# Weight conversions in a spectral mixing stage: six in place of five, their absolute value moved ahead of the relu, matrix loads at other units

## The chip, the core and the metric

The kernel runs on one core of a Trainium2 chip. The metric is the device time of one execution in microseconds (us), the median over several runs. Engines are named as the profile names them: PE (TensorE matmul), PEld (its weight loads), DVE (VectorE), ACT (ScalarE), POOL (GpSimd), SP (SyncE, which here only issues transfers). Every engine works through its own list of instructions in order, and waits on semaphores for the others.

## What is computed

The input is `x` of 2 x 3008 x 256 (batch, sequence, dim). A spectral stage takes a real Fourier transform along the sequence, mixes the 256 channels by one complex matrix with bias, shrinks real and imaginary part softly towards zero, and transforms back. Two feed-forward layers follow.

```python
X = np.fft.rfft(x, axis=1)
Yr = Xr @ w_r - Xi @ w_i + b_r
Yi = Xr @ w_i + Xi @ w_r + b_i
Yr = np.sign(Yr) * np.maximum(np.abs(Yr) - 0.01, 0.0)   # Yi likewise
y = np.fft.irfft(Y, n=x.shape[1], axis=1)
h = y @ w_in;  g = h * sigmoid(1.702 * h);  z = g @ w_out     # 256 -> 2048 -> 256
h = z @ w_in2; g = h * sigmoid(h);          out = g @ w_out2
```

The four feed-forward matrices arrive as 64-bit floats, seen by the kernel as pairs of 32-bit words.

## The kernel before, in words

The work runs in five stages: the forward transform (`fwd`), the mixing (`mid`), the inverse transform (`inv`), and the two feed-forward layers (`mlp`). In all of them the order of each engine's instructions is the order in which the code is written; no scheduler moves them.

**The mixing** has twelve units `i` = 0 to 11 (two batches, two parities of frequency, three blocks of 128 frequencies). PE does a unit into two PSUM banks (`mid_mm`, L539, L542); from unit 2 on that is 25 matmuls of 512 columns, 12 into the first bank, closed by a bias matmul (L545), then 12 into the second. Units from 2 on work on `x` split into a high part `xh` (ACT, L482) and a low part `xl` (ACT, L478, then a POOL-issued transfer that adds, L479). Banks of even units come from pool `ps0`, of odd units from `ps1`, four banks each, so unit `i` needs the banks of unit `i-4` back; the inverse uses the same pools.

Behind PE, one loop pass `i` treats the unit before: ACT copies the first bank to `us` (L551), DVE forms sums and differences of both banks, `sd` (L553 to L555, which frees the banks), ACT applies the relu (L561), DVE finishes the shrinkage `th` (L566), and one pass later DVE folds it to `f` (L578), which the inverse multiplies. The same pass also splits `x` for units `i+2` and `i+3`.

**A weight conversion** (`cv_bits`, L169) turns one 128 x 512 block of 64-bit weights into float32. It has one raw buffer, one work buffer `cv_c`, and these steps: ACT takes the absolute value of the upper words (L175, `cv_c<-raw`), which needs the raw block landed and `cv_c` free again; DVE does five bit operations (L180 to L184); POOL issues a transfer that adds `cv_c` onto `cv_a` in memory (L185), and SP loads the next raw block. `cv_c` is free for the next conversion only when that adding transfer has landed. The DVE and POOL steps wait in a list `fill`, which `pump()` writes out at chosen places. `window(k, done)` places finished blocks (`place_in`, `place_out`: sums on DVE, split into high and low part) and begins `k` new conversions.

Ten of the 32 conversions stand ahead of `mlp`: three in `fwd` (`tf`), those at the units in `tm` in `mid`, those at the steps in `ti` in `inv`. The table `li` says at which units one of the inverse's four matrix pairs (0.8 to 1.2 MB, tiles `m`) is loaded by SP; the fourth is loaded at step 0 of `inv`. SP's list has both these and the raw blocks. Before the change the loop ends, for `i` in `tm`, with placing and beginning a conversion, so that L175 stands behind the relu of pass `i` and its DVE work in pass `i+1`.

**The inverse** has 16 steps (q, b, t). PE does a step (`inv_mm`, L376) into two banks; a step later ACT copies one bank to `eo` (L668) and DVE combines them into `rt` (L672, L676, L406) or adds and subtracts them (L687, L688). The list `pl` says at which steps a converted block, popped from the list `hold`, is placed. The result `yt` is split into `x` blocks for the first feed-forward layer.

**The feed-forward layers** are matmuls L836 (first product, a fast 2 x 2 scheme) and L808 (second product).

Of the kernel before, what the change touches and what calls it, by code (L numbers as in the profile page):

```python
# [8 lines left out]

F32 = mybir.dt.float32  # L10
CFG = {'lv0': 'V', 'lv': 'V', 'dd0': 'VPVVPPPPPVVP', 'dd': 'V', 'ths': 'VVVVPV', 'thf': 'V', 'ivf': 'V', 'cva': 'P', 'pol': 'PPPP', 'pil': 'P', 'mvl': 'PVVP', 'xl': 'V', 'xse': 'V', 'gl': 'VPPPPPPP', 'tf': [6, 10, 13], 'tm': [1, 3, 5, 7, 9], 'ml': [], 'pk': 6, 'ti': [3, 7], 'pi': 4, 'pl': [1, 4, 8, 10, 13], 'kb': [0, 1, 1, 1, 1, 1, 1, 0], 'kr': [0, 1, 0, 1, 0, 1, 1, 0], 'fa': 3, 'xp': [2, 4, 4, 5], 'xq': [1, 4, 1], 'xs': 4, 'xi': [7, 7, 9, 10, 10, 11, 8], 'xsi': 9, 'xo': (0, 1, 6, 2, 3, 4, 5), 'xd': (0, 1, 4, 6), 'ca': 4, 'tl': True, 'fwd': 'all', 'rest0': 'all', 'rest1': 'all', 'last1': 'all', 'inv': 'all', 'mid': 'all', 'last0': 'all', 'thm': 'A', 'gl0': 'PVPVVVPV', 'gl2': 'PPPPPPPP', 'gl3': 'PPPPPPPV', 'xl0': 'VVVVVPV', 'xl1': 'V', 'pre': 13, 'pre2': 0, 'yd': 6, 'lvb': 6, 'mlp': 'all', 'pr': 'V', 'pf': 'V', 'eo': '0111', 'n32': 2, 'li': [8, 10, 11], 'lii': [0], 'xa': 4, 'nhb': 6, 'ddb': 6, 'mlp1': 'all', 'mlp2': 'all'}
NUM = dict(li=[5, 6, 7, 8], n32=2, pk=4, ydp=2, lii=[1, 3], xd=(), ml=[], pl=[], xo=range(7), pi=6, nhb=6, tf=[5, 9, 13], tm=[1, 3, 5, 7, 9, 11], ti=[0, 2, 4, 6, 8, 10, 12, 14, 14, 15, 15], kb=[2] * 8, kr=1, fa=3, fe=2, pm=0, nf=4, lvb=6, ddb=8, ivb=1, eob=1, fsb=6, f1=3, f2=0, fm=[7, 8, 9], fi=[1, 1, 2, 2], pre=13, pre2=1, yd=3, psh=0, ie=[12], xp=[1, 3, 4, 5], xq=[1, 2, 2], xs=5, nw=4, xi=[14, 14, 15, 15], xsi=13, rw=2, ca=4, cc=2, tb=1, tmn=1)

DEF = dict(pr="V", pf="V", lv0="V", lv="VPP", dd0="VVVVVP", dd="VPV", mpl="PV", ths="VP", thf="VVPP", fsl="VP", ivf="PPVV", cva="P", pol="P", pil="P", mvl="V", xl="PPVVPPP", xl0="PPVVPPP", xl1="PPVVPPP", xse="VP", gl="P", gl0="P", gl2="P", gl3="P", wcl="V", thc="V", thm="V")
# [42 lines left out]
def spectral_mlp_kernel(ctx, tc, xin, mfwd, minv, wc, bias, w_in1, w_out1, w_in2, w_out2, outT):  # L57
# [4 lines left out]
    def N(k):  # L62
        return CFG.get(k, NUM[k])
# [102 lines left out]
                nc.sync.dma_start(out=raw[:, :].rearrange("p (r d) -> p r d", r=2), in_=src)  # L166
            loaded.append(((kind, l, p, kept), raw))

    def cv_bits(raw, tag="a"):  # L169
        w = raw.bitcast(U32).rearrange("p (n t) -> p n t", t=2)  # L170
        hf = raw.bitcast(F32).rearrange("p (n t) -> p n t", t=2)[:, :, 1]
        c = cv_p.tile([P, 2 * CU], F32, tag="c", name="cv_c", bufs=1)
        a = cv_p.tile([P, 2 * CU], F32, tag=tag, name="cv_a", bufs=3 if tag == "a" else 1)
        cu, au = c.bitcast(U32), a.bitcast(U32)
        nc.scalar.activation(c, hf, AF.Abs, scale=2.0**-112)  # L175
        ts, stt = nc.vector.tensor_scalar, nc.vector.scalar_tensor_tensor
        band, bor, shl = ALU.bitwise_and, ALU.bitwise_or, ALU.logical_shift_left
# [57 lines left out]
    def settle(now=False):  # L235
        pump()
        ended[:] = []
        for u, (a, c) in bits:
            if not u[3]:
                spilled[u[:3]] = d = dram_p.tile([P, 2 * CU], F32, name=f"w_{u[0]}{u[1]}_{u[2]}")  # L240
                nc.sync.dma_start(out=d, in_=a)
        fresh = [(u, a) for u, (a, _) in bits if u[3]]
        done, added[:] = (added + fresh, ()) if now else (added[:], fresh)
        bits[:] = []
        return done

    def window(k, done, now=False, tag="a"):
        for u, a in done:
            if u[0] == "in":
                sums, puts = place_in(u[1], u[2], a, nc.vector if u[2] == NPR // 2 else "D", sums_tmp)  # L250
                if now:
                    for f in (puts[0], *sums, puts[1]):
                        f()
                else:
                    fill.extend(sums + puts)
            else:
                place_out(u[1], u[2], a, nc.gpsimd if u[2] == NPR - 2 else "D")
        for _ in range(min(k, len(loaded))):
            u, raw = loaded.pop(0)
            bits.append((u, cv_bits(raw, tag)))  # L260

    def tick(k=1):
        window(k, settle(True))
# [327 lines left out]
    for i in range(len(mids)):  # L591
        ps = mid_mm(i)
        sd = mid_sd(*post) if post is not None else None
        xsplit(i + 3, 1)
        xsplit(i + 2, 0)
        if thr is not None:
            mid_fold(*thr)
        if sd is not None:
            thr = mid_relu(*sd)
            pump()  # L600
            thr = mid_th(*thr)
        if i in N('li'):
            load_m()
        post = (i, ps)
        if i in N('tm'):
            ready = settle(True)
            window(0, [r for r in ready if r[0][2] < NPR // 2 and r[0][0] == "in"])
            hold.extend(r for r in ready if r[0][2] >= NPR // 2 or r[0][0] == "out")
            window(1, (), tag="ld" if i == N('tm')[-1] else "a")
    sd = mid_sd(*post)  # L610
    mid_fold(*thr)
    thr = mid_relu(*sd)
    pump()
    mid_fold(*mid_th(*thr))
# [516 lines left out]
```

## Time and profile before

| | us |
|---|---|
| median of 3 runs (lowest, highest) | 1166.54 (1165.54, 1167.99) |
| the profiled execution, own time | 1166.52 |
| its span in the trace | 1164.7 |
| PE busy in the span | 1146.9 |
| ACT / DVE / POOL busy | 774.4 / 629.7 / 477.9 |
| mean granted TensorE clock | 0.995 of full |

The span is what the trace covers; 1.8 us of the execution lie around it. A PE that is busy for 98 per cent of the span still may wait in one place, so the stretch around the edit has to be read by itself. Times in the rows are counted from the span's start: the mixing's matmuls run from 61.9 to 132.9, the inverse's from there to 190, then the feed-forward layers to the end.

### The profile page before, as it was taken

The page shows a single profiled execution, that of the slowest core. Times are in us where ns is not written, and L with a number is a line of the kernel's source. Part 1 is how long each engine was busy: PE and PEld are TensorE (multiplying, and loading weights), DVE is VectorE, ACT ScalarE, POOL GpSimd, SP SyncE. Part 2 cuts the span into 40 slices and gives each one's busy share as a digit, 9 for nine tenths or more (in the row PEclk, how much of TensorE's full clock was granted, in tenths as well). Part 3 has the DMA queues.
Part 4 walks back from the last instruction along what each step waited for, and adds up shares of the span by engine and source line. Part 5 has one row for each costly group of instructions (what it writes and reads, how often), then busy time and mean ns, then how long its engine had stood idle before and what let it go on. Part 6 is the DMA issues. An engine that isn't in the chain of part 4 may idle for free.

```text
span 1164.7 us, 14637 instructions
## 1 busy us (share of the span) xinstructions
PE 1146.9 (98%) x5094; PEld 949.7 (82%) x5094; DVE 629.7 (54%) x1013; ACT 774.4 (66%) x1444; POOL 477.9 (41%) x412
## 2 busy tenths in 40 slices
PE   8999899999999999999999999999999999999998
PEld 6768786887888888888889878888888888888897
DVE  7777798766365474575563553442533523523522
ACT  2576446877677667676677786665766765766755
POOL 1243134454444443444436655333433333433333
PEclk9999899999999999999999999999999999999999
DMA  8777666451121121211220100000000000000000
GB/s 295 179 142 149 149 149 119 109 113 33 49 72 37 36 73 37 60 49 37 72 55 19 55 19 19 1 37 1 1 37 1 30 7 1 37 1 1 37 1 32
DMA packets 39564, 68.49 MB, mean 59 GB/s; under 512 B 3649, under 2 KB 15809, under 8 KB 39490
## 3 DMA queue, kind: packets, MB, share of 16 engines
q1 hardware_dynamic: 26162, 45.51, 11.9%
q0 software_dynamic: 13328, 22.05, 11.2%
q8 instruction: 40, 0.66, 0.2%
q14 instruction: 34, 0.28, 0.1%
HBM read 35.15 MB, written 10.35 MB: 39 GB/s over the span
## 4 chain that ended last, share of the span: by engine, by line
PE 81%; issue 7%; ACT 3%; DVE 3%; DMA 3%; POOL 2%; SPq 0%; POOLq 0%; DVEq 0%; ACTq 0%
PE o L808 40%; PE x L836 35%; PE psf L376 4%; PE psm L539 1%; ACT yt L839 1%; DMA cv_a<-cv_c 1%; DMA wo<-cv_a 1%; POOL xl L479 1%; ACT g L841 1%; DMA raw<-in_x 1%; DVE yt L858 0%; DMA xl<-xt 0%; POOL yt L722 0%; ACT x L747 0%; DVE yt L887 0%
## 5 line engine op out<-in xcount | busy, mean ns | idle before, releaser
L846 POOL TENSOR_TENSOR g<-yt,g 128x512 fp32r<-128x512 f32 (+1 forms) x282 | 362.7, 1298 | 495.8 <-PE x L836 332.0
L808 PE MATMUL o<-g,wo 128*128 128x512 f32 (+1 forms) x2304 | 560.1, 385 | 0.5 <-DMA wo<-cv_a 0.5
L836 PE MATMUL x<-x,wi 128*128 128x512 f32 (+1 forms) x2016 | 498.8, 386 | 3.5 <-ACT yt L877 1.9
L808 PEld LDWEIGHTS o<-g,wo 128*128 128x128 f32 x2304 | 432.4, 188 | 81.5 <-DMA wo<-cv_a 1.0
L836 PEld LDWEIGHTS x<-x,wi 128*128 128x128 f32 x2016 | 377.0, 188 | 80.4 <-ACT yt L877 4.9
L839 ACT ACTIVATE yt<-yt 128x512 f32<-128x512 f32 (+1 forms) x288 | 179.1, 622 | 253.6 <-DVE yt L887 204.8
L841 ACT CAST g<-yt 128x512 fp32r<-128x512 f32 (+1 forms) x384 | 235.1, 612 | 12.2
L887 DVE TENSOR_TENSOR yt<-yt,x 128x512 f32<-128x512 f32 (+1 forms) x96 | 64.7, 674 | 214.3 <-PE x L836 213.7
L858 DVE TENSOR_TENSOR yt<-yt,x 128x512 f32<-128x512 f32 (+1 forms) x96 | 64.8, 675 | 167.1 <-ACT yt L855 165.2
L846 DVE TENSOR_TENSOR g<-yt,g 128x512 fp32r<-128x512 f32 (+1 forms) x102 | 70.1, 687 | 73.2 <-ACT g L841 73.2
L185 POOL DMA_DIRECT2D cv_a<-cv_c x32 | 28.1, 877 | 98.4 <-DVE cv_c L184 92.0
L891 DVE TENSOR_TENSOR yt<-yt,x 128x512 f32<-128x512 f32 (+1 forms) x96 | 64.8, 674 | 0.4 <-issue 0.3
L754 DVE TENSOR_TENSOR x<-yt,x 128x512 fp32r<-128x512 f32 (+1 forms) x44 | 46.2, 1051 | 29.6 <-ACT x L747 29.6
L875 ACT COPY yt<-x 128x512 f32<-128x512 f32 (+1 forms) x96 | 54.7, 570 | 2.9 <-PE x L836 2.9
L839 ACT ACTIVATE yt<-x 128x512 f32<-128x512 f32 (+1 forms) x96 | 56.1, 584 | 0.0
L877 ACT COPY yt<-x 128x512 f32<-128x512 f32 (+1 forms) x96 | 55.7, 580 | 0.1
L376 PE MATMUL psf<-m,xf 128*128 128x190 f32 (+3 forms) x224 | 53.2, 399 | 2.4 <-POOL xf L327 2.4
L376 PE MATMUL psi<-m,f 128*128 128x188 f32 (+3 forms) x224 | 49.0, 373 | 6.2 <-DVE sd L555 2.9
L855 ACT COPY yt<-x 128x512 f32<-128x512 f32 (+1 forms) x96 | 54.7, 570 | 0.0
L376 PEld LDWEIGHTS psf<-m,xf 128*128 128x128 f32 x224 | 39.3, 193 | 16.1 <-POOL xf L327 3.0
L376 PEld LDWEIGHTS psi<-m,f 128*128 128x128 f32 x224 | 39.7, 199 | 13.8 <-DVE sd L555 3.2
L175 ACT ACTIVATE cv_c<-raw 128x512 f32<-128x512 f32 x32 | 21.5, 673 | 19.0 <-DMA cv_a<-cv_c 8.7
(118 smaller groups left out, 817.5 us busy)
## 6 DMA issues: line engine op xcount, KB each, us to landing
raw<-in_wi SPq DMA_DIRECT2D x32, 256.0 KB, 3.7
cv_a<-cv_c POOLq DMA_DIRECT2D x32, 256.0 KB, 5.1
raw<-in_wo SPq DMA_DIRECT2D x16, 512.0 KB, 3.9
xl<-xt POOLq DMA_DIRECT2D x20, 256.0 KB, 4.3
out_t<-yt SPq DMA_DIRECT2D x20, 256.0 KB, 2.0
raw<-in_x SPq DMA_DIRECT2D x9, 512.0 KB, 6.0
w_in<-cv_a SPq DMA_DIRECT2D x8, 256.0 KB, 2.0
w_out<-cv_a SPq DMA_DIRECT2D x8, 256.0 KB, 2.0
```

The source lines that it names most:

```text
L376: nc.tensor.matmul(ps, hi[:, c : c + P], m[:, k, :w], start=i == 0, stop=i == last)
L808: nc.tensor.matmul(acc[h, mm], st, mv, start=first and k == 0, stop=last and k == 2)
L836: nc.tensor.matmul(ps, st, mv, start=first and m == 0, stop=m == 2, skip_group_check=True)
L839: nc.scalar.activation(g, g if src is None else src, func)
L841: nc.scalar.copy(gh, g)
L846: eng.tensor_sub(gl, g, r32(gh))
L855: nc.scalar.copy(y1, X)
L858: nc.vector.tensor_add(y1, y1, Y)
L875: nc.scalar.copy(y2, Z)
L877: nc.scalar.copy(y3, X)
L887: nc.vector.tensor_add(y2, y2, X)
L891: nc.vector.tensor_add(y3, y3, Z)
```

## The change

In the mixing, conversions begin at units 0, 2, 4, 6, 8, 10 in place of 1, 3, 5, 7, 9, and in the inverse at step 3 alone in place of 3 and 7; the total stays at ten ahead of `mlp`. The block that places and begins is moved from the end of the pass to the place between the splits and `mid_fold`. `pump()` runs in every pass, pass 0 too. The sixth conversion writes into a slot of the pool that holds `x`. The first of the placed blocks with index 4 has its low part made by ACT and an adding transfer (`"D"`) in place of two DVE subtractions. The matrices are loaded at units 3, 5, 7 in place of 8, 10, 11. The sixth block is put third in `hold`.

```diff
-CFG = {... 'tm': [1, 3, 5, 7, 9], ... 'ti': [3, 7], ... 'li': [8, 10, 11], ...}
+CFG = {... 'tm': [0, 2, 4, 6, 8, 10], ... 'ti': [3], ... 'li': [3, 5, 7], ...}
...
-    def cv_bits(raw, tag="a"):
+    def cv_bits(raw, n):
...
-        a = cv_p.tile([P, 2 * CU], F32, tag=tag, name="cv_a", bufs=3 if tag == "a" else 1)
+        if n < 4:
+            a = cv_p.tile([P, 2 * CU], F32, tag="a", name="cv_a", bufs=3)
+        elif n == 4:
+            a = cv_p.tile([P, 2 * CU], F32, tag="ld", name="cv_a", bufs=1)
+        else:
+            a = slot(0, F32, "cv_a")
...
-                sums, puts = place_in(u[1], u[2], a, nc.vector if u[2] == NPR // 2 else "D", sums_tmp)
+                sums, puts = place_in(u[1], u[2], a, "D", sums_tmp)
...
         xsplit(i + 3, 1)
         xsplit(i + 2, 0)
+        if i in N('tm'):
+            ready = settle(True)
+            window(0, [r for r in ready if r[0][2] < NPR // 2 and r[0][0] == "in"])
+            hold.extend(r for r in ready if r[0][2] >= NPR // 2 or r[0][0] == "out")
+            window(1, (), n=N('tm').index(i))
         if thr is not None:
             mid_fold(*thr)
         if sd is not None:
             thr = mid_relu(*sd)
-            pump()
+        pump()
+        if sd is not None:
             thr = mid_th(*thr)
         if i in N('li'):
             load_m()
         post = (i, ps)
-        if i in N('tm'):
-            ready = settle(True)
-            window(0, [r for r in ready if r[0][2] < NPR // 2 and r[0][0] == "in"])
-            hold.extend(r for r in ready if r[0][2] >= NPR // 2 or r[0][0] == "out")
-            window(1, (), tag="ld" if i == N('tm')[-1] else "a")
...
     hold.extend(settle(True))
+    hold.insert(2, hold.pop())
```

PE's list of instructions is the same in both, row by row. Three places show what moves. Line numbers of the changed kernel are 5 to 7 higher than before.

First ACT, in passes 9 to 11 of the mixing, from the copy of unit 8's bank to that of unit 11's (`us` is the copy, `th` the relu, `cv_c<-raw` the absolute value that begins a conversion). Before:

```order
L551 COPY us<-psm 128x512
L482 CAST xh<-xt_318 128x512
L482 CAST xh<-xt_319 128x512
L561 ACTIVATE th<-sd,neglam 128x512 x2
L175 ACTIVATE cv_c<-raw_1173 128x512
L551 COPY us<-psm 128x512
L561 ACTIVATE th<-sd,neglam 128x512 x2
L551 COPY us<-psm 128x512
L561 ACTIVATE th<-sd,neglam 128x512 x2
L551 COPY us<-psm 128x512
```

The same passes in the changed kernel:

```order
L556 COPY us<-psm 128x512
L487 CAST xh<-xt_318 128x512
L487 CAST xh<-xt_319 128x512
L566 ACTIVATE th<-sd,neglam 128x512 x2
L556 COPY us<-psm 128x512
L180 ACTIVATE cv_c<-raw_1193 128x512
L566 ACTIVATE th<-sd,neglam 128x512 x2
L556 COPY us<-psm 128x512
L566 ACTIVATE th<-sd,neglam 128x512 x2
L556 COPY us<-psm 128x512
```

The absolute value stood between the relu of pass 9 and the copy of unit 9's bank; it now stands behind that copy and ahead of the relu of pass 10.

Second DVE in the inverse, around the outputs of its second batch (`yt<-rt`) and the first `x` block's preparation. Before:

```order
L718 TENSOR_TENSOR yt<-rt 128x2x187
L180 TENSOR_SCALAR cv_c<-cv_c 128x512
L181 TENSOR_SCALAR cv_c<-cv_c 128x512
L182 SCALAR_TENSOR_TENSOR cv_a<-raw_1478,cv_c 128x512
L183 TENSOR_SCALAR cv_c<-cv_a 128x512
L672 TENSOR_TENSOR rt<-psi,eo 128x2x188
L406 TENSOR_TENSOR rt<-psi,eo 128x2x188
```

The same place in the changed kernel:

```order
L725 TENSOR_TENSOR yt<-rt 128x2x187
L679 TENSOR_TENSOR rt<-psi,eo 128x2x188
L411 TENSOR_TENSOR rt<-psi,eo 128x2x188
L744 TENSOR_TENSOR tmp<-yt 128x512
L745 TENSOR_TENSOR yt<-yt 128x512
```

The second conversion of the inverse is gone from here; a conversion more stands at the start of the mixing instead.

Third SP, from the first matrix load on (`m<-in_mi`; `raw` are the blocks of weights). Before:

```order
L166 DMA raw_1058<-in_wo 128x2x256
L166 DMA raw_1173<-in_wo 128x2x256
L137 DMA m<-in_mi 128x768 x2
L166 DMA raw_1275<-in_wo 128x2x256
L137 DMA m<-in_mi 128x760 x2
L137 DMA m<-in_mi 128x752 x2
L137 DMA m<-in_mi 128x1128 x2
```

The same place in the changed kernel:

```order
L137 DMA m<-in_mi 128x768 x2
L166 DMA raw_954<-in_wo 128x2x256
L137 DMA m<-in_mi 128x760 x2
L166 DMA raw_1075<-in_wo 128x2x256
L137 DMA m<-in_mi 128x752 x2
L166 DMA raw_1193<-in_wo 128x2x256
L166 DMA raw_1292<-in_wo 128x2x256
L137 DMA m<-in_mi 128x1128 x2
```

Three matrix pairs now stand each directly behind a raw block, two raw blocks earlier than before and more.

## Rows read from the trace of the kernel before

**Rows 1.** The page, busy time and share of the span, by engine:

```profile
PE 1146.9 (98%) x5094; PEld 949.7 (82%) x5094; DVE 629.7 (54%) x1013; ACT 774.4 (66%) x1444; POOL 477.9 (41%) x412
```

**Rows 2.** PE's timeline, 132.9 to 197: start, length, operation, idle before and releaser:

```profile
132.91 4.06 PE L376 MATMUL psi<-m,f 128*128 128x192 f32 x24
139.91 2.93 PE L376 MATMUL psi<-m,f 128*128 128x192 f32 x8 [2.94 <-DVE sd L555]
143.30 1.64 PE L376 MATMUL psi<-m,f 128*128 128x190 f32 x4 [0.46 <-DMA m<-in_mi]
...
162.93 15.65 PE L376 MATMUL psi<-m,f 128*128 128x188 f32 x72 [1.27 <-DVE rt L406]
179.32 1.54 PE L376 MATMUL psi<-m,f 128*128 128x188 f32 x8 [0.74 <-DVE rt L406]
181.69 4.06 PE L376 MATMUL psi<-m,f 128*128 128x376 f32 x12 [0.82 <-DVE rt L688]
185.93 0.96 PE L836 MATMUL x<-x,wi 128*128 128x512 f32 x3 [0.19 <-ACT eo L668]
...
195.25 2.34 PE L836 MATMUL x<-x,wi 128*128 128x512 f32 x9 [0.85 <-DVE yt L887]
```

**Rows 3.** Windows: length, then busy by engine, granted clock, DMA share, GB/s:

```profile
139.91:148.94 9.03, 8.57 (x35) 8.06 (x35) 8.93 (x16) 2.93 (x6) 0.00 (x0) 0.66 1.01 338
148.94:161.66 12.72, 12.72 (x79) 12.43 (x78) 11.72 (x25) 4.01 (x7) 3.41 (x3) 1.00 0.18 36
...
162.93:178.58 15.65, 15.65 (x72) 12.16 (x72) 14.98 (x30) 10.87 (x21) 9.84 (x10) 1.00 1.12 187
```

**Rows 4.** PE's timeline, the bias matmul of unit 9:

```profile
118.60 0.39 PE L545 MATMUL psm<-bias_hl,ones 128*128 128x512 f32 x1
```

**Rows 5.** ACT's timeline in the mixing, absolute values and one copy:

```profile
71.27 0.66 ACT L175 ACTIVATE cv_c<-raw 128x512 f32<-128x512 f32 x1
...
116.76 0.67 ACT L175 ACTIVATE cv_c<-raw 128x512 f32<-128x512 f32 x1 [2.58 <-DMA cv_a<-cv_c]
...
130.96 0.66 ACT L175 ACTIVATE cv_c<-raw 128x512 f32<-128x512 f32 x1 [4.52 <-DMA cv_a<-cv_c]
131.53 0.57 ACT L551 COPY us<-psm 128x512 f32<-128x512 f32 x1
```

**Rows 6.** DVE's timeline at the end of the mixing and in the inverse:

```profile
134.60 0.42 DVE L180 TENSOR_SCALAR cv_c<-cv_c 128x512 f32<-128x512 f32 x1
...
136.70 0.69 DVE L184 SCALAR_TENSOR_TENSOR cv_c<-raw,cv_c 128x512 f32<-128x512 uint32 x1
...
139.44 0.42 DVE L555 TENSOR_TENSOR sd<-psm,us 128x256 f32<-128x256 f32 x1
...
142.18 0.68 DVE L553 TENSOR_TENSOR sd<-us,psm 128x512 f32<-128x512 f32 x1
...
148.63 0.55 DVE L676 TENSOR_TENSOR rt<-psi,eo 128x380 f32<-128x380 f32 x1
...
154.44 0.55 DVE L110 TENSOR_TENSOR wi<-cv_a,wi 128x384 fp32r<-128x384 f32 x1
...
162.33 0.55 DVE L406 TENSOR_TENSOR rt<-psi,eo 128x376 f32<-128x376 f32 x1
```

**Rows 7.** POOL's timeline, adding transfers of conversions:

```profile
60.90 0.85 POOL L185 DMA_DIRECT2D cv_a<-cv_c  x1 [0.65 <-DVE cv_c L184]
...
111.25 0.86 POOL L185 DMA_DIRECT2D cv_a<-cv_c  x1 [4.47 <-DVE cv_c L184]
...
123.50 0.86 POOL L185 DMA_DIRECT2D cv_a<-cv_c  x1 [3.03 <-DVE cv_c L184]
137.69 0.86 POOL L185 DMA_DIRECT2D cv_a<-cv_c  x1 [13.32 <-DVE cv_c L184]
```

**Rows 8.** SP's timeline, the first matrix load:

```profile
123.69 0.47 SPq L137 DMA_DIRECT2D m<-in_mi  x1
```

**Rows 9.** Groups by line, one of the four sums of a placed block:

```profile
L213 DVE TENSOR_TENSOR tmp<-cv_a 128x128 f32<-128x128 f32 x8 | 2.3, 285 | 0.5 <-DMA cv_a<-cv_c 0.5
```

More of the change, by code (lines that the diff above doesn't have):

```diff
@@ L10 @@
 F32 = mybir.dt.float32
-CFG = {'lv0': 'V', 'lv': 'V', 'dd0': 'VPVVPPPPPVVP', 'dd': 'V', 'ths': 'VVVVPV', 'thf': 'V', 'ivf': 'V', 'cva': 'P', 'pol': 'PPPP', 'pil': 'P', 'mvl': 'PVVP', 'xl': 'V', 'xse': 'V', 'gl': 'VPPPPPPP', 'tf': [6, 10, 13], 'tm': [1, 3, 5, 7, 9], 'ml': [], 'pk': 6, 'ti': [3, 7], 'pi': 4, 'pl': [1, 4, 8, 10, 13], 'kb': [0, 1, 1, 1, 1, 1, 1, 0], 'kr': [0, 1, 0, 1, 0, 1, 1, 0], 'fa': 3, 'xp': [2, 4, 4, 5], 'xq': [1, 4, 1], 'xs': 4, 'xi': [7, 7, 9, 10, 10, 11, 8], 'xsi': 9, 'xo': (0, 1, 6, 2, 3, 4, 5), 'xd': (0, 1, 4, 6), 'ca': 4, 'tl': True, 'fwd': 'all', 'rest0': 'all', 'rest1': 'all', 'last1': 'all', 'inv': 'all', 'mid': 'all', 'last0': 'all', 'thm': 'A', 'gl0': 'PVPVVVPV', 'gl2': 'PPPPPPPP', 'gl3': 'PPPPPPPV', 'xl0': 'VVVVVPV', 'xl1': 'V', 'pre': 13, 'pre2': 0, 'yd': 6, 'lvb': 6, 'mlp': 'all', 'pr': 'V', 'pf': 'V', 'eo': '0111', 'n32': 2, 'li': [8, 10, 11], 'lii': [0], 'xa': 4, 'nhb': 6, 'ddb': 6, 'mlp1': 'all', 'mlp2': 'all'}
+CFG = {'lv0': 'V', 'lv': 'V', 'dd0': 'VPVVPPPPPVVP', 'dd': 'V', 'ths': 'VVVVPV', 'thf': 'V', 'ivf': 'V', 'cva': 'P', 'pol': 'PPPP', 'pil': 'P', 'mvl': 'PVVP', 'xl': 'V', 'xse': 'V', 'gl': 'VPPPPPPP', 'tf': [6, 10, 13], 'tm': [0, 2, 4, 6, 8, 10], 'ml': [], 'pk': 6, 'ti': [3], 'pi': 4, 'pl': [1, 4, 8, 10, 13], 'kb': [0, 1, 1, 1, 1, 1, 1, 0], 'kr': [0, 1, 0, 1, 0, 1, 1, 0], 'fa': 3, 'xp': [2, 4, 4, 5], 'xq': [1, 4, 1], 'xs': 4, 'xi': [7, 7, 9, 10, 10, 11, 8], 'xsi': 9, 'xo': (0, 1, 6, 2, 3, 4, 5), 'xd': (0, 1, 4, 6), 'ca': 4, 'tl': True, 'fwd': 'all', 'rest0': 'all', 'rest1': 'all', 'last1': 'all', 'inv': 'all', 'mid': 'all', 'last0': 'all', 'thm': 'A', 'gl0': 'PVPVVVPV', 'gl2': 'PPPPPPPP', 'gl3': 'PPPPPPPV', 'xl0': 'VVVVVPV', 'xl1': 'V', 'pre': 13, 'pre2': 0, 'yd': 6, 'lvb': 6, 'mlp': 'all', 'pr': 'V', 'pf': 'V', 'eo': '0111', 'n32': 2, 'li': [3, 5, 7], 'lii': [0], 'xa': 4, 'nhb': 6, 'ddb': 6, 'mlp1': 'all', 'mlp2': 'all'}
 NUM = dict(li=[5, 6, 7, 8], n32=2, pk=4, ydp=2, lii=[1, 3], xd=(), ml=[], pl=[], xo=range(7), pi=6, nhb=6, tf=[5, 9, 13], tm=[1, 3, 5, 7, 9, 11], ti=[0, 2, 4, 6, 8, 10, 12, 14, 14, 15, 15], kb=[2] * 8, kr=1, fa=3, fe=2, pm=0, nf=4, lvb=6, ddb=8, ivb=1, eob=1, fsb=6, f1=3, f2=0, fm=[7, 8, 9], fi=[1, 1, 2, 2], pre=13, pre2=1, yd=3, psh=0, ie=[12], xp=[1, 3, 4, 5], xq=[1, 2, 2], xs=5, nw=4, xi=[14, 14, 15, 15], xsi=13, rw=2, ca=4, cc=2, tb=1, tmn=1)
@@ L245, in settle, with window @@
         return done
-    def window(k, done, now=False, tag="a"):
+    def window(k, done, now=False, n=0):
         for u, a in done:
             if u[0] == "in":
-                sums, puts = place_in(u[1], u[2], a, nc.vector if u[2] == NPR // 2 else "D", sums_tmp)
+                sums, puts = place_in(u[1], u[2], a, "D", sums_tmp)
                 if now:
@@ L259, in window @@
             u, raw = loaded.pop(0)
-            bits.append((u, cv_bits(raw, tag)))
+            bits.append((u, cv_bits(raw, n)))
     def tick(k=1):
```

## The prediction, as it was put on record

> **What bounds the kernel now.** I read the page first: PE is busy for 98% of the span, all other engines for two thirds or less [rows 1]. PE's list of instructions is untouched, so the change can only alter how long PE stands still, or at which clock it runs. PE's own timeline says where that is. Between the mixing's last matmul (132.9) and the first feed-forward matmuls (195) it stops seven times [rows 2]. The largest stop is at the seam: the second step of the inverse waits 2.94 us for DVE's L555, the last op that reads unit 10's banks, and then 0.46 for a matrix. Later it waits 1.27 and 0.74 for L406, 0.82 for L688, 0.19 for ACT's `eo` copy, and 0.85 for L887. After the 2.94 us of idling the granted clock falls to a mean of 0.66 of full over 139.91 to 148.94, part of it at 1.2 in place of 2.4 GHz [rows 3]. There 35 matmuls took 8.57 us; in the next window 79 of nearly the same width took 12.72, 0.161 each, so 35 should take 5.64 and the slow clock cost 2.93.
>
> **Why DVE is late at the seam.** In PE's row for unit 9 the first bank is complete at 118.60 + 0.39 = 118.99 [rows 4]. ACT copies it at 131.53, 12.5 us later, though the copy waits for nothing but its turn: right ahead stands L175, the absolute value, idle for 4.52 us until an adding transfer has freed `cv_c` [rows 5]. Behind that copy come unit 9's sums, folds, and on DVE the five conversion ops from 134.60 to 136.70 + 0.69 = 137.39, the shrinkage, and unit 10's sums, done at 139.44 + 0.42 = 139.86 [rows 6]. PE starts at 139.91. DVE leaves the mixing at 148.63 and is then busy without a break (14.98 of 15.65 us in 162.93 to 178.58, [rows 3]); the 1.27, 0.74 and 0.82 are its lateness carried on.
>
> **The new rhythm.** A conversion round is: absolute value 0.66, the DVE ops 2.79, 0.30 until POOL issues at 137.69, then a tail until the next absolute value may run. Where that one waited for the tail, it was 5.51 (111.25 to 116.76) and 7.46 (123.50 to 130.96) [rows 5, 7]. Before, another 3.64 stood inside the round (130.96 to 134.60): the copy, sums and folds queued between the absolute value and L180. The change puts these ahead of the absolute value, so they can run while it waits. A round thus costs 9.26 to 11.21, mid 10.24, against two PE units of 11.36 (from 118.60 to 132.91 are 63 matmuls, 2.52 units, so 5.68 each).
>
> Six absolute values are five rounds. The first needs the last forward conversion's transfer, issued at 60.90 [rows 7]: 66.4 to 68.4 by the same tails, and at most 71.27, when it ran without waiting [rows 5]. I take 68.4. Two rounds carry the four sums of a placed block, 4 x 0.285 = 1.14 each [rows 9]. The sixth is then at 68.4 + 51.2 + 2.3 = 121.9; with all tails long and the late start 71.3 + 56.1 + 2.3 = 129.7. The tail I choose is the mean of the two, because three of five rounds have matrix loads beside them: the long tail had one, issued at 123.69 [rows 8], the short one none.
>
> What the Trainium skill says of this speaks against the change: "DMA: Bandwidth & Descriptors", section "Queues, rings and completion order", has each transfer engine serve its queues in turn, packet by packet, so a matrix load on SP's queue shares time with POOL's adding transfer beside it and does not wait behind it. The two tails agree with it, without proving it. By it the three rounds with matrices would take the long tail and the rest the short one, 68.4 + 52.2 + 2.3 = 122.9.
>
> **When it is early enough.** From the absolute value to unit 10's sums done there is 0.66 + (139.86 - 134.60) = 5.92, and from there to DVE's first op of the inverse 148.63 - 139.86 = 8.77, the same ops as before: the inverse begins on DVE 14.69 behind the sixth absolute value. It cannot begin before unit 11's own sums allow: they need PE's last matmul (132.9), and took 148.63 - 142.18 = 6.45 to get there, so 139.4. The tightest need of PE behind it is the second half of step 8 (8 of its 16 matmul rows stand before the 1.27 us stop, 8 behind), which waits for the last reader of a bank of step 4: done at 162.33 + 0.55 = 162.88, that is 14.25 into DVE's inverse. The subtractions that leave DVE (0.55 for 384 columns, the second for 512 not shown, about 0.7, less overlap: 1.1) make that 13.15. PE running freely is there at 132.91 + (8 x 16 + 8) x 0.161 = 154.8. So DVE must begin by 141.6, and the sixth absolute value must run by 127.0. My 121.9 leaves 5.1 us, the floor of 139.4 leaves 2.2. Each microsecond past 127.0 costs one.
>
> Steps 13 and 14, where PE waited 0.74 and 0.82 for the readers of steps 9 and 10, get slack from the removed conversion: its five ops (2.8 us) stood on DVE among those readers. The 0.46 for the matrix goes because its load now stands on SP behind the raw block that pass 2 asks for, and not where it was issued at 123.69. The 0.19 goes with the rest, as the ACT copy follows PE and DVE.
>
> **Edits costed at nothing.** The conversion in pass 0 adds 1.14 + 2.79 = 3.9 us of DVE, and the ACT work of a placed block, while PE does units 0 and 1; PE first feels it if unit 3's splits or unit 4's banks (those of unit 0) come late, units later. In4's low part goes to a transfer that is not needed until the fifth feed-forward group. The sixth block's slot is taken from one of `x`'s early units, all read by then, and given back at step 8. If one of these covers fails, the cost is a wait of PE in the mixing, up to some microseconds, which I hold in the range. The 0.85 for L887 stays: it is the feed-forward layer's own chain.
>
> **Sum.** 2.94 + 0.46 + 2.93 + 1.27 + 0.74 + 0.82 + 0.19 = 9.35 us. The profiled execution took 1166.52, the median is 1166.54, so nothing is to be scaled: 1166.5 - 9.35 = 1157.2.
>
> **Rivals.** *Late rounds (0.14).* If all tails are long, the sixth absolute value is at 129.7, 2.7 past the point: 1159.9. For it: the matrices' 2.3 MB move from the seam into the mixing. Against: even so PE's first stop (unit 10's sums, at 135.6 in place of 139.86) is gone.
>
> *Gain given back in the inverse (0.10).* The transfers are at a share of 1.12 in 162.93 to 178.58 [rows 3] and nearly the same ones must pass while PE is 9 us quicker. They start earlier by as much as DVE does (148.63 - 139.4 = 9.2), so they have no room to spare; if `x` blocks then come 2 to 3 us late, 1159 to 1160.
>
> *Slower (0.05).* The rounds do not shorten: four rounds from 71.27 to 130.96 are 14.92 each, and now there are five. The sixth absolute value would be at 68.4 + 74.6 = 143.0, 16.0 past the point: 1173.2, more if the clock falls again. For it: each absolute value waited for a transfer, which moving it does not make faster. Against: 3.64 of the last round was queue, not transfer. It decides from rounds of about 13.6 us (68.4 + 5 x 13.6 = 136.4, 9.4 past the point) on.
>
> *No change (0.03).* Losses and gains within 0.2% of each other, 2.3 us, which is about what a measurement here can tell from nothing.
>
> **The numbers.** Forecast 0.68, which with the late rounds and the give-back makes faster by over 0.2% 0.91; same 0.04, slower 0.05. Range: the low end takes away the 0.85 too, and 0.4 for run spread, 1155.9; the high end takes in the late rounds with 0.7 for a tail longer than the two seen, 1160.6. Outside lie the slower cases, no change, and bits of the rest, about 0.15 to 0.2.
>
> **What would show it.** Right: no stop of PE between 132.9 and 139; granted clock 1.00 in 140 to 149; sixth absolute value before 127.0; DVE's first L676 op (then L683) near 139.5; first feed-forward matmuls near 176.6 in place of 185.93; PE's timeline after that the same, shifted by 9.35. Wrong: rounds above 11.4 us; stops of PE for L406 at step 8; a stop in the mixing around units 3 to 5 for `xh` or `xl`; `x` matmuls waiting for transfers.

## The result and the profile after

The changed kernel takes 1155.38 us in the median of 4 runs (1154.44 to 1156.45). Beside it the kernel before took 1167.26 (1165.54 to 1168.42). The ratio is 0.9900, with a 95% interval of 0.9882 to 0.9918: faster by about 1%, 11.9 us by the medians. The forecast was 1157.2 with a range of 1155.9 to 1160.6, so direction and place came as forecast, and the gain was larger than the range allowed. The profiled execution of the changed kernel took 1156.45 (span 1154.6), 10.07 less than that of the kernel before.

The page of the changed kernel, busy time by engine (to be read beside [rows 1]):

```profile
PE 1141.8 (99%) x5094; PEld 946.6 (82%) x5094; DVE 629.1 (54%) x1011; ACT 775.7 (67%) x1446; POOL 478.8 (41%) x414
```

PE's timeline of the changed kernel over the stretch of [rows 2], from the first matmul of the inverse to the wait for the `x` sums:

```profile
133.26 6.01 PE L381 MATMUL psi<-m,f 128*128 128x192 f32 x36
...
142.63 6.97 PE L381 MATMUL psi<-m,f 128*128 128x190 f32 x42
...
152.95 22.68 PE L381 MATMUL psi<-m,f 128*128 128x190 f32 x106
175.18 1.14 PE L843 MATMUL x<-x,wi 128*128 128x512 f32 x3
...
184.69 2.33 PE L843 MATMUL x<-x,wi 128*128 128x512 f32 x9 [0.85 <-DVE yt L894]
```

Of seven stops one is left, the 0.85 for L894 (L887 before). From the first row to that last one it takes 184.69 - 133.26 = 51.43 us; before it was 195.25 - 132.91 = 62.34 [rows 2]. I call this "the stretch" below. It is 10.91 shorter. The profiled execution of the changed kernel began the stretch 0.35 later, and by the difference of the own times lost 0.49 more behind it: 10.91 - 0.35 - 0.49 = 10.07.

To see where the 10.91 lie, the stretch is cut at four places that are the same in PE's list. Windows of the kernel before (columns as in [rows 3]: the first figure behind the window is its length, the third from the end the granted clock):

```profile
132.91:148.94 16.03, 12.63 (x60) 11.83 (x58) 15.79 (x30) 5.41 (x9) 0.86 (x1) 0.79 0.65 209
148.94:162.93 13.99, 12.72 (x79) 12.43 (x78) 12.96 (x28) 4.01 (x7) 3.72 (x3) 1.00 0.26 46
162.93:185.93 23.00, 21.25 (x92) 15.61 (x92) 22.12 (x43) 15.63 (x31) 15.46 (x16) 1.00 1.11 195
185.93:195.25 9.32, 8.47 (x30) 5.45 (x30) 7.99 (x16) 5.59 (x10) 3.25 (x4) 1.00 0.77 133
```

The same four pieces of PE's list in the changed kernel:

```profile
133.26:142.63 9.37, 9.37 (x60) 9.37 (x59) 8.31 (x15) 3.17 (x6) 0.21 (x1) 1.00 0.30 113
142.63:155.19 12.56, 12.56 (x80) 12.56 (x80) 12.18 (x28) 4.94 (x9) 6.36 (x7) 1.00 0.66 98
155.19:175.18 19.99, 19.99 (x93) 15.59 (x93) 17.70 (x34) 13.86 (x27) 13.26 (x15) 1.00 1.04 181
175.18:184.69 9.51, 8.66 (x33) 5.52 (x31) 7.91 (x16) 5.40 (x10) 3.54 (x5) 1.00 0.66 107
```

Saved: 6.66 at the seam (forecast 2.94 + 0.46 + 2.93 = 6.33), 1.43 around step 8 (forecast 1.27), 3.01 in the rest of the inverse (forecast 0.74 + 0.82 + 0.19 = 1.75), and 0.19 lost in the last piece, at the matmuls right behind the cut. The clock is 1.00 throughout. Each of the first three pieces gave back more than its visible idle time; over the whole stretch it is 10.91 - 9.35 = 1.56 us more.

ACT's timeline of the changed kernel, the absolute values of the six conversions (beside [rows 5]):

```profile
67.07 0.68 ACT L180 ACTIVATE cv_c<-raw 128x512 f32<-128x512 f32 x1 [0.68 <-DMA raw<-in_wi]
...
78.14 0.68 ACT L180 ACTIVATE cv_c<-raw 128x512 f32<-128x512 f32 x1 [2.20 <-DMA raw<-in_wi]
...
90.33 0.67 ACT L180 ACTIVATE cv_c<-raw 128x512 f32<-128x512 f32 x1 [0.64 <-DMA raw<-in_wi]
...
102.05 0.68 ACT L180 ACTIVATE cv_c<-raw 128x512 f32<-128x512 f32 x1 [1.00 <-DMA cv_a<-cv_c]
...
114.30 0.66 ACT L180 ACTIVATE cv_c<-raw 128x512 f32<-128x512 f32 x1 [1.85 <-DMA cv_a<-cv_c]
...
122.97 0.67 ACT L180 ACTIVATE cv_c<-raw 128x512 f32<-128x512 f32 x1 [1.48 <-DMA cv_a<-cv_c]
```

And POOL's, the adding transfers of the first five (beside [rows 7]):

```profile
70.88 0.86 POOL L190 DMA_DIRECT2D cv_a<-cv_c  x1 [0.64 <-DVE cv_c L189]
...
83.18 0.86 POOL L190 DMA_DIRECT2D cv_a<-cv_c  x1 [0.64 <-DVE cv_c L189]
...
94.13 0.86 POOL L190 DMA_DIRECT2D cv_a<-cv_c  x1 [4.32 <-DVE cv_c L189]
106.47 0.86 POOL L190 DMA_DIRECT2D cv_a<-cv_c  x1 [5.30 <-DVE cv_c L189]
118.09 0.86 POOL L190 DMA_DIRECT2D cv_a<-cv_c  x1 [5.52 <-DVE cv_c L189]
```

The rounds are 11.07, 12.19, 11.72, 12.25 and 8.67, where the four rounds of before were 14.92 in the mean. The sixth absolute value runs at 122.97. From a POOL row to the next ACT row it is 7.26, 7.15, 7.92, 7.83 and 4.88. The last three of these ended with the adding transfer; the third and fourth have a matrix load beside them, the fifth has none. The first two ended with the landing of the raw block (`raw<-in_wi` in ACT's rows), and the first of them has no matrix load beside it.

DVE's timeline of the changed kernel, its first operation of the inverse and the last reader of step 4's banks:

```profile
139.99 0.55 DVE L683 TENSOR_TENSOR rt<-psi,eo 128x380 f32<-128x380 f32 x1
...
152.63 0.55 DVE L411 TENSOR_TENSOR rt<-psi,eo 128x376 f32<-128x376 f32 x1
```

The reader is done at 153.18; PE comes to the second half of step 8 at 155.19, so there are 2.01 us to spare. (The expectations below say 155.03 and 1.85, which is one matmul too early: 155.19 is the 137th of the inverse, as 162.93 is in [rows 2].)

### The profile page after: what moved, and what is told of

Read it like the earlier page. It is cut to its first block, busy times and chain, and to the rows that moved or that the text cites. A ratio compares the mean times of both kernels' runs of the same rounds, so it can differ in the third digit from the quotient of the medians.

```text
span 1154.6 us, 14648 instructions
## 1 busy us (share of the span) xinstructions
PE 1141.8 (99%) x5094; PEld 946.6 (82%) x5094; DVE 629.1 (54%) x1011; ACT 775.7 (67%) x1446; POOL 478.8 (41%) x414
## 4 chain that ended last, share of the span: by engine, by line
PE 94%; ACT 2%; DVE 1%; issue 1%; DMA 1%; POOL 0%; SPq 0%; POOLq 0%; DVEq 0%
PE o L815 42%; PE x L843 37%; PE psm L547 5%; PE psf L381 4%; PE psi L381 4%; PE psm L544 1%; ACT yt L846 1%; DMA raw<-in_x 1%; ACT x L754 0%; DVE yt L865 0%; DMA wo<-cv_a 0%; DVE x L761 0%; ACT g L848 0%; ACT yt L862 0%; PE psm L550 0%
## 5 line engine op out<-in xcount | busy, mean ns | idle before, releaser
L894 DVE TENSOR_TENSOR yt<-yt,x 128x512 f32<-128x512 f32 (+1 forms) x96 | 64.8, 675 | 214.3 <-PE x L843 213.8
L381 PE MATMUL psi<-m,f 128*128 128x188 f32 (+3 forms) x224 | 45.1, 357 | 0.0
L754 ACT CAST x<-tmp 128x512 fp32r<-128x512 f32 (+1 forms) x36 | 22.1, 613 | 17.4 <-DVE tmp L763 15.8
```

What stands on the lines that cost most here:

```text
L381: nc.tensor.matmul(ps, hi[:, c : c + P], m[:, k, :w], start=i == 0, stop=i == last)
L894: nc.vector.tensor_add(y2, y2, X)
```

## The experiments

All are edits of the changed kernel unless said otherwise; none changes what is computed. "The stretch" is read in each trace as above (51.43 in the changed kernel; 51.42 in its second trace).

**The changed kernel twice more**, as the level for the others.

> The changed kernel itself, as the level for the others on the same chip. Both theories: 1155.4 us give or take 1.0. If the 1.6 us beyond the forecast were only the luck of the first comparison, the difference to the kernel before should now come near 9.4 us; if they are lost around the stops in time that the profile does not count as idle, near 11 us (10.9 in the two traces between the mixing's last matmul and the wait for the x sums, 11.1 between the fastest runs).

> The changed kernel itself, as the level of this chip for the other two: 1154.4 to 1156.5, in two levels by the granted clock at the start.

Measured: 1154.47 (1154.38 to 1154.68) against 1167.3 for the kernel before, ratio 0.9898 (0.9883 to 0.9912); and 1154.88 (1154.45 to 1156.15) against 1167.48, ratio 0.9897 (0.9881 to 0.9914). So the excess over the forecast was no luck of one comparison: by medians the gain is 11.9 to 12.8 us.

**The place undone.**

```diff
         xsplit(i + 2, 0)
-        if i in N('tm'):
-            ready = settle(True)
...
             thr = mid_relu(*sd)
-        pump()
-        if sd is not None:
+            pump()
             thr = mid_th(*thr)
...
         post = (i, ps)
+        if i in N('tm'):
+            ready = settle(True)
...
```

> Everything of the change but the place: the six conversions begin at the end of the pass again, behind the relu, and the fill list is written out where it was. Theory (the place in ACT's and DVE's lists sets the length of a round): rounds of about 14.9 us as before, the sixth absolute value at 68.4 + 5 x 14.9 = 143, the sums of unit 10 5.9 us later at 149, PE stops for them from about 137 on, 10 to 12 us, and the granted clock falls again: about 1173 us, slower than before. Rival (one conversion less in the inverse, the earlier start and the moved matrices bring the gain, the place does not): 1155 to 1158 us.

Measured: 1166.06 (1164.18 to 1168.32), ratio to the kernel before 0.9991 (0.9980 to 1.0002), no difference beyond the noise. The whole gain is lost without the place. The expected time, 1173, was 7 us too long. ACT's timeline of this kernel shows the rounds and the queue (`us` is the copy of a finished bank):

```profile
124.99 0.66 ACT L180 ACTIVATE cv_c<-raw 128x512 f32<-128x512 f32 x1 [4.57 <-DMA cv_a<-cv_c]
125.56 0.57 ACT L556 COPY us<-psm 128x512 f32<-128x512 f32 x1
...
136.59 0.66 ACT L180 ACTIVATE cv_c<-raw 128x512 f32<-128x512 f32 x1 [1.93 <-DMA cv_a<-cv_c]
137.15 0.57 ACT L556 COPY us<-psm 128x512 f32<-128x512 f32 x1
```

The first four rounds are 14.99, 15.03, 14.25 and 14.23, as the theory says, but the fifth only 11.60, so the sixth absolute value runs at 136.59 and not at 143. The two last tails, from POOL's issue on, are 7.50 (117.49 to 124.99, a matrix load issued at 117.69) and 4.87 (131.72 to 136.59, none), which is the 2.63 by which the fifth round is shorter. The matrix load is not all that differs: two adding transfers of `xl` also stand behind the first of the two (118.03) and none behind the second. It is in matrices_late, below, that a matrix load alone is put beside the last tail. PE's stops in its timeline:

```profile
137.77 3.60 PE L381 MATMUL psi<-m,f 128*128 128x192 f32 x20 [2.38 <-ACT us L556]
...
145.53 0.59 PE L381 MATMUL psi<-m,fd 128*128 128x190 f32 x2 [0.96 <-DVE sd L560]
...
151.77 7.69 PE L381 MATMUL psi<-m,f 128*128 128x192 f32 x28 [3.38 <-DVE rt L411]
```

PE's first stop now ends with the copy that stands right behind the late absolute value (137.15 + 0.57 = 137.72, PE at 137.77): the queue, not the conversion's own work, holds it up. Windows of the same kernel:

```profile
137.00:141.00 4.00, 3.23 (x19) 3.11 (x20) 3.21 (x7) 2.58 (x5) 0.00 (x0) 1.00 0.00 0
150.00:154.00 4.00, 2.23 (x7) 2.23 (x8) 3.31 (x9) 1.30 (x3) 0.86 (x1) 0.60 0.24 99
```

After the stop of 2.38 the clock stayed at 1.00, after that of 3.38 it fell.

**The place alone.**

```diff
-'tm': [0, 2, 4, 6, 8, 10], 'ti': [3],    'li': [3, 5, 7]
+'tm': [1, 3, 5, 7, 9],     'ti': [3, 7], 'li': [8, 10, 11]
-                sums, puts = place_in(u[1], u[2], a, "D", sums_tmp)
+                sums, puts = place_in(u[1], u[2], a, nc.vector if u[2] == NPR // 2 else "D", sums_tmp)
-    hold.insert(2, hold.pop())
```

> The place alone: the five conversions of before at units 1, 3, 5, 7, 9 and two in the inverse, matrices at units 8, 10, 11, the DVE subtractions kept; only where a conversion begins and where the fill list is written out are as in the changed kernel. Theory: the fifth absolute value runs near 71.3 + 4 x 11 = 115, long before the seam, so the 2.94 us stop, the slow clock and the stop at step 8 go; the removed conversion is back on DVE in the inverse (2.8 us) and may bring back 0.7 to 1.6 us around steps 13 and 14: 1155.4 to 1158. Rival (it takes the conversion out of the inverse, or the matrices out of the seam): 1161 us or more.

Measured: 1156.71 (1156.25 to 1158.30), ratio 0.9918 (0.9904 to 0.9932), 10.6 us faster than the kernel before beside it. Its PE timeline has two stops besides that for the `x` sums:

```profile
171.10 4.06 PE L381 MATMUL psi<-m,f 128*128 128x376 f32 x12 [0.82 <-DVE rt L694]
175.35 0.98 PE L842 MATMUL x<-x,wi 128*128 128x512 f32 x3 [0.19 <-ACT eo L674]
...
184.70 2.34 PE L842 MATMUL x<-x,wi 128*128 128x512 f32 x9 [0.85 <-DVE yt L893]
```

The seam is clean; the inverse's second conversion brings back the stop of step 14. No stop for a matrix came back, though the loads are at their old units. The stretch is 184.70 - 131.33 = 53.37, 1.95 longer, though the profile counts only 1.01 as idle. So the place is worth 10.6 of 12.8 us by the medians. The rest comes with the other edits together; of these, the matrices and the subtractions cost nothing clear in the time when undone alone (below), which leaves the sixth conversion. The place in ACT's list and the place in DVE's move together in this edit, and no run parts them.

**Six conversions, each a unit later.**

```diff
-'tm': [0, 2, 4, 6, 8, 10]
+'tm': [1, 3, 5, 7, 9, 11]
```

> The changed kernel with the six conversions at units 1, 3, 5, 7, 9, 11 in place of 0, 2, 4, 6, 8, 10. Theory: the first absolute value at about 71.3, rounds as in the changed kernel (56 us for five), the sixth at about 127, at the point from which on PE waits; behind it fewer sums are queued than I counted, so 1155.4 to 1157. Rival (the earlier start by a unit is what the gain rests on): 4 to 5 us of it are lost, 1159 to 1161 us.

Measured: 1156.57 (1154.59 to 1156.95), ratio 0.9909 (0.9892 to 0.9925). The sixth absolute value ran at 128.31, 1.3 us past the prediction's 127.0, and yet there was no stop at step 8; DVE began the inverse at 140.49, 12.18 behind it and not 14.69. The stretch was 51.95, with one stop of 0.19: the delay of a whole unit costs 0.5 us. The rest of the distance of the medians stands ahead of the stretch, which in this trace begins at 132.86 (131.35 in the changed kernel's second trace). The rival's 4 to 5 us aren't there.

**The matrices back at their old units.**

```diff
-'li': [3, 5, 7]
+'li': [8, 10, 11]
```

> The changed kernel with the matrix loads back at units 8, 10, 11. Theory (they only free the seam of the 0.46 us wait, and lie beside long tails wherever they are): the rounds with units 3 to 7 get shorter by up to 3 us each, the sixth absolute value comes before 122, PE then either waits again about 0.5 us for a matrix near the seam or not at all, since the raw blocks ahead of them on SP now come earlier too: the time within 1 us of the changed kernel's (1154.4 to 1156.4). Rival (moving the matrices carries a good part of the gain, as loads beside the seam hold up the conversions there): 1158 us or more.

Measured: 1154.97 (1154.28 to 1156.72), ratio 0.9898 (0.9883 to 0.9913), and a stretch of 51.42. Moving them brought nothing, once the raw blocks come earlier. But the rounds did not get shorter by up to 3 us each, as I had expected. ACT's timeline of this kernel:

```profile
78.86 0.67 ACT L180 ACTIVATE cv_c<-raw 128x512 f32<-128x512 f32 x1 [2.15 <-DMA raw<-in_wi]
...
89.59 0.68 ACT L180 ACTIVATE cv_c<-raw 128x512 f32<-128x512 f32 x1 [0.16 <-DMA cv_a<-cv_c]
...
100.69 0.66 ACT L180 ACTIVATE cv_c<-raw 128x512 f32<-128x512 f32 x1
...
112.10 0.68 ACT L180 ACTIVATE cv_c<-raw 128x512 f32<-128x512 f32 x1
...
123.85 0.68 ACT L180 ACTIVATE cv_c<-raw 128x512 f32<-128x512 f32 x1 [4.08 <-DMA cv_a<-cv_c]
```

The three rounds that lost their matrix load take 10.73, 11.10 and 11.41, shorter by 1.46, 0.62 and 0.84. The last, with a load issued at 116.46 beside its tail, takes 11.75, longer by 3.08; its tail is 7.58 (from POOL's issue at 116.27) in place of 4.88, and the sixth absolute value runs at 123.85 and not before 122. The absolute values at 100.69 and 112.10 waited for no transfer. Their distance is 11.41, two units of PE (11.36): a conversion stands two passes behind the last, each of these passes begins with the copy of a bank and with splits of `x` that wait for PE (0.72 and 0.73 ahead of 100.69), and so a short tail is not used. The last pass with a conversion has no `x` left to split, and there a late round can catch up: the 8.67 of the changed kernel.

**The subtractions back on DVE.**

```diff
-                sums, puts = place_in(u[1], u[2], a, "D", sums_tmp)
+                sums, puts = place_in(u[1], u[2], a, nc.vector if u[2] == NPR // 2 else "D", sums_tmp)
```

> The changed kernel with the low part of the first block with index 4 made by two DVE subtractions again (about 1.1 us of DVE in the inverse). Theory: in the changed kernel's trace the reader of step 4 is done at 153.18 and PE comes to it at 155.03, 1.85 us later, so 1.1 us more on DVE costs nothing: within 0.5 us of the changed kernel. Rival (the point is tighter, and this edit is a needed part of the gain): 1 us or more is lost in one stop at step 8.

Measured: 1155.05 (1154.53 to 1156.81), ratio 0.9900 (0.9885 to 0.9916), the same as the changed kernel; the stretch is 52.08, 0.66 longer, with one stop of 0.19 for ACT's `eo`, none at step 8. The slack at step 8 is as read; the cost came at the end of the inverse.

**Needless work on DVE ahead of the inverse**: six, then nine additions.

```diff
     mid_fold(*mid_th(*thr))
+    wt = tmp()
+    for _ in range(6):                   # 9 in the second kernel
+        nc.vector.tensor_add(wt, ft[0, 0, 0, 0], ft[0, 0, 0, 0])
```

> The changed kernel with six additions of 512 columns that nobody needs (0.69 us each, 4.1 in all) on DVE ahead of its first operation of the inverse. Theory, first part: the slack at step 8 is 1.85 us, so PE gets one stop of about 2.3 us there. Second part: a stop costs more than the idle time that the profile gives, by 0.16 to 0.4 us, so the stretch from the inverse's first matmul to the wait for the x sums grows by 2.4 to 2.7 (51.43 to about 54.0). The granted clock stays at 1.00, as it did after a stop of 2.38 in the kernel with the old place. Rival to the first: DVE is not what PE waits for there, nothing changes. Rival to the second: the stretch grows by just the idle time shown.

> As the kernel with six needless additions on DVE, but nine of them (6.2 us). With six, the stretch from the inverse's first matmul to the wait for the x sums grew from 51.42 to 55.30, by 3.88, of which the profile counted 2.65 as idle. Theory: from here on each microsecond on DVE costs one, so three additions more (2.07) make it 57.4, if no single stop is long enough for the granted clock to fall; the rise of the first stop (0.35) and that at step 8 (1.49) share it. If one stop comes to 3 us, as at the seam before, the clock falls to 0.50 for some microseconds and the stretch is 60 to 61. Rival (a fixed price per stop, nothing in proportion): 55.3 to 56.

With six: 1159.10 (1157.86 to 1160.17). PE's timeline of that kernel:

```profile
131.21 6.01 PE L381 MATMUL psi<-m,f 128*128 128x192 f32 x36
...
143.35 4.81 PE L381 MATMUL psi<-m,f 128*128 128x192 f32 x28 [0.35 <-DVE rt L411]
...
155.41 16.90 PE L381 MATMUL psi<-m,f 128*128 128x188 f32 x80 [1.49 <-DVE rt L411]
172.93 4.06 PE L381 MATMUL psi<-m,f 128*128 128x376 f32 x12 [0.62 <-DVE rt L698]
177.18 0.97 PE L846 MATMUL x<-x,wi 128*128 128x512 f32 x3 [0.19 <-ACT eo L678]
...
186.51 2.35 PE L846 MATMUL x<-x,wi 128*128 128x512 f32 x9 [0.85 <-DVE yt L897]
```

Four stops, not one, of 0.35 + 1.49 + 0.62 + 0.19 = 2.65 in all. The stretch is 55.30, 3.88 longer, at a clock of 1.00. So 1.23 us are lost without being shown as idle. Set beside the changed kernel's second trace start by start, each of the four stops delays PE by 0.27 more than its idle time, and the remaining 0.14 lies at two matmuls in front of which no idle time is shown. The second part of the theory holds, and the rival that only the idle time counts falls. Of the first part the place holds (L411 at step 8, the largest), the count does not.

With nine: 1162.29 (1159.79 to 1165.23), a stretch of 57.53 where 57.4 was expected for an undisturbed clock. But the clock fell all the same, so the agreement does not confirm the reasoning. PE's one large stop:

```profile
147.27 6.49 PE L381 MATMUL psi<-m,f 128*128 128x192 f32 x28 [2.54 <-DVE rt L411]
```

and a window behind it:

```profile
148.00:150.00 2.00, 2.00 (x8) 2.00 (x7) 1.93 (x7) 0.69 (x3) 0.86 (x1) 0.50 0.03 5
```

Here the stop at step 8 is gone. One reading is that PE at 1.2 GHz came to step 8 late enough that DVE was done, so slow clock and stop stood in for each other; the trace is consistent with that, no run held the clock apart.

**The start.** The profiled executions of the changed kernel differ ahead of the stretch. A window of the changed kernel's first trace:

```profile
12.00:14.00 2.00, 2.00 (x4) 1.00 (x3) 1.51 (x3) 0.51 (x3) 0.42 (x5) 0.50 1.07 405
```

The same window of its second trace:

```profile
12.00:14.00 2.00, 2.00 (x8) 1.21 (x7) 1.15 (x3) 0.64 (x4) 0.20 (x4) 1.00 1.02 395
```

In the first PE ran 4 matmuls there at half clock, in the second 8, and the stretch began at 133.26 and 131.35; the own times are 1156.45 and 1154.42. Two kernels add warming matmuls: seven more ahead of the first pair (the first two lines of the diff), or five between the first pairs (the rest).

```diff
-    for _ in range(13):
+    for _ in range(20):
         nc.tensor.matmul(warm[:, :P], ones_f, ones_f, start=True, stop=True)
...
+    between = [3, 2]
...
+            for _ in range(between.pop(0) if i and between else 0):
+                nc.tensor.matmul(warm[:, :P], ones_f, ones_f, start=True, stop=True)
```

> The changed kernel with 20 in place of 13 warming matmuls at the start. This is about the spread of the runs: the changed kernel's executions come at 1154.4 and at 1156.4, and in the traces the second kind has a granted clock of 0.50 over 12 to 14 us while the first has 1.00. Theory (what differs is the start, where PE stands idle between the first blocks): the warming, some 3 us longer, fills the idle time up to the second pair of matmuls at 8.5 to 9.3, the clock stays at 1.00, and all executions are near 1154.4, or up to 1 us more where the first matmuls come late. Rival (the two levels come from elsewhere): both are still there, or the time is 1 to 3 us longer.

> The changed kernel with three warming matmuls between the first and the second pair of matmuls at the start, and two between the second and the third, where PE stood idle for 0.9 to 2.8 and 0.5 to 1.1 us. Theory (the two levels of the changed kernel, 1154.4 and 1156.4, are the granted clock at the start, which falls after these pauses): clock 1.00 over 10 to 16 us, and all executions between 1154.2 and 1155.2. Rival (the level does not hang on the pauses; a longer warming ahead of the first pair left executions at 1155.3 and 1156.2): the spread stays at about 2 us. If the inserted matmuls come late themselves, up to 1 us is added to all.

Measured: 1154.61 (1154.17 to 1156.16) and 1154.50 (1154.15 to 1154.97), ratios 0.9894 and 0.9893 with intervals that cover the changed kernel's. With the longer warming the higher executions are still there; with the one between the pairs they were absent in 4 runs, which the unedited kernel also did once. That the start makes the levels is shown by the traces; that the pauses alone decide it is not: one_unit_later lost the clock after pauses of 1.08 and 0.51, after_third kept it after 2.77 and 0.57.

The same five matmuls in the kernel before:

> The kernel before with the same five warming matmuls between the first pairs at the start. In all runs so far the kernel before lies between 1164.6 and 1170.6 us, the changed one between 1154.3 and 1156.7. Theory (the changed kernel varies by its start alone; the kernel before varies by its start and by up to 4 us at the seam, where the stops and the slow clock hang on when transfers land): with the start held at clock 1.00 its lowest time stays at 1164 to 1165, its highest falls by about 2 to 1168 or 1169, so it still spreads over 3 us or more, and its median comes to 1165 to 1167. Rival (all of its spread is the start, too): all executions within about 1 us, near 1164.5.

Measured: 1166.27 (1164.63 to 1167.70), against 1167.38 (1165.61 to 1170.35) without. The spread stays at 3.1 us, so it is not the start's alone. In its trace the stretch begins 1.15 earlier than in the other trace of before (131.76), and the wait for the `x` sums ends at 195.18, only 0.07 earlier. The lead was not lost at the seam: PE comes to the second half of step 8 at 161.26, 1.67 earlier than the 162.93 of [rows 2]. It was lost behind that, where the clock fell after stops of 1.06 (at 178.09) and 0.82:

```profile
180.45 5.67 PE L378 MATMUL psi<-m,f 128*128 128x376 f32 x12 [0.82 <-DVE rt L691]
```

```profile
180.00:182.00 2.00, 1.55 (x3) 0.97 (x4) 1.93 (x5) 0.09 (x2) 1.56 (x2) 0.58 1.01 266
```

The same row took 4.06 in the other trace [rows 2]. So the two ends agree by chance. That the seam is what spreads the kernel before, as the theory has it, these two traces do not show: the seam's piece, cut as above, takes 16.03 in one and 16.36 in the other (131.76 to 148.12).

## Why the gain was larger than forecast, step by step

*The cause of the stall* (the place of the conversion, with its absolute value ahead of the copy in ACT's queue) was right, and shown: undoing the place alone takes away the whole gain, the place alone brings 10.6 of 12.8 us.

*The rhythm*: the sixth absolute value was forecast at 121.9 and measured at 122.97, by errors that cancel. The first came 1.33 earlier (67.07 for 68.4). From each absolute value to POOL's issue the five rounds take 20.86 together, forecast 5 x 3.75 + 2.3 = 21.05. The tails behind POOL's issue take 35.04 together, forecast 5 x 6.485 = 32.43 (the mean of 5.51 and 7.46), because four were long and one short. What I missed is the raw block: it ended the first two rounds, at 7.26 and 7.15, and the sum has no term for it. Three of the rounds lay above 11.4, which the prediction calls a sign of being wrong; it cost nothing here, as the sixth absolute value still had 4 us to spare. What the Trainium skill says of queues served in turn ("DMA: Bandwidth & Descriptors", section "Queues, rings and completion order") agrees with the tails that end with the adding transfer, 7.92, 7.83 and 4.88, and with 7.58 where a matrix load was moved beside the last one in matrices_late. By it I had worked out 122.9; that the trace gives 122.97 is luck, as it has four long tails where I counted three, and the earlier start.

*The point from which lateness costs* was right for DVE (by 141.6): DVE began at 139.99, and the measured reader and PE put the point at 139.99 + 2.01 = 142.00, with the inverse begun 0.35 later. For the absolute value (by 127.0) it was too early: in one_unit_later 128.31 brought no stop at step 8, because DVE's work behind it took at most 12.18 and not 14.69. The rival of late rounds did not come, nor did the transfers give anything back: their share is 1.04 over 155.19 to 175.18, and no `x` block was late. The slower rival is refuted with its price: even with the old place it is 1166. There the rounds were as long as feared, but for the last.

*Edits costed at nothing*: the conversion in pass 0, the slot of `x` and in4's transfer cost PE nothing in the mixing, which has no stop. The matrices' move was worth nothing, where I had given it the 0.46.

*The step that failed is the sum.* It priced a stop at the idle time in front of PE's row. In running work the next matmul starts before the last has ended: groups by line and form of the changed kernel give

```profile
L381 PE MATMUL psi<-m,f 128*128 128x188 f32 x88 | 15.5, 322 | 0.0
```

322 ns for one (the profile models the ends), while 42 of nearly that width take 6.97, (6.97 - 0.32) / 41 = 0.162 from one start to the next. The profile counts idle time from the end of the last matmul, 0.16 after the next one should have started, and behind a stop the second start is late as well. PE's timeline of the kernel before has two matmuls behind the stop of 1.27 as

```profile
162.93 0.59 PE L376 MATMUL psi<-m,f 128*128 128x188 f32 x2 [1.27 <-DVE rt L406]
```

and that of the changed kernel two in running work as

```profile
140.70 0.48 PE L381 MATMUL psi<-m,f 128*128 128x188 f32 x2
```

Both pairs end with a matmul of 0.32, so the second start lies 0.27 behind the first in one pair and 0.16 in the other. Set beside each other start by start, the two traces give 0.27 more than the idle time for each of the four stops behind the seam, 0.16 for each of the two at the seam (there the late second start is part of the slow clock's 2.93), and 0.16 at two matmuls where no idle time is shown: 4 x 0.27 + 2 x 0.16 + 0.16 = 1.56. dve_plus_4 shows the same 0.27 a stop with nothing else changed. The Trainium skill says why, in "TensorE: Matmul & The Clock Gate", section "Step-by-step: what each phase is for": the drain of one matmul lies under the fill of the next, and only one without a successor shows it. The rows agree, with 0.16 of 0.32 overlapped. With 9.35 + 1.56 = 10.91, less the 0.35 and 0.49 outside the stretch, the trace's 10.07 is reached.

*The low end of the range* failed by the run spread as well: 0.4 us, where the start alone moves executions by 2. The profiled execution of the changed kernel, 1156.45, lies inside the range; the median lies 1.07 below it. The profiled execution of before was one with the clock at 0.50 near 10 to 12 us, so its 1166.52 less 9.35 held that loss, which half of the changed kernel's four executions beside it, by their times, do not have. And the kernel before lies between 1164.62 and 1170.59 over all runs, the changed one between 1154.38 and 1156.45 over its twelve: with the stops goes a source of spread, and the medians gain up to 2.8 us more than the two traces. How much of that lies in the stops and how much in the clock that falls behind them stays open.

## What to carry to other kernels

Where an engine's queue holds an instruction that waits for a transfer, look at what stands behind it: moving it one place back, behind what others need, can be worth more than shortening the wait. Price a stop of PE from start to start of its matmuls, never by the idle time alone, and compare the same pieces of its list in both traces. A chain that is issued once per n passes, behind work that waits for PE, runs no faster than n passes as long as it keeps up, however short its parts; only one that has fallen behind can catch up.

## What had not been expected of the hardware

The granted clock did not follow the length of one pause alone: it stayed at 1.00 after 2.38 us (old_place_six) and 2.77 (after_third's start), and fell after 2.54 (dve_plus_6), 2.94 [rows 2] and, at a start, after pauses of 1.08 and 0.51 (one_unit_later). In before_warm_between it fell after stops of 1.06 and 0.82, and stayed at 1.00 in the other trace of that kernel after 0.74 and 0.82 in front of the same matmuls. And two equal ends can hide different losses: the kernel before reached 195.2 us whether its inverse began at 132.91 or 131.76, once with the clock at 1.00 behind step 8 and once with a fall there.
